# A fused long convolution and Mish MLP on one core: new order of the front, transposing DMAs for ten token tiles, and a column-tiled last hidden chunk

## The chip, the cores and the metric

The kernel runs on one core of one Trainium2 chip. The metric is device time in microseconds (us) of one execution, lower is better. A profiled execution has a span, from its first to its last recorded instruction, and a time of its own, which is a little longer.

## The reference, cut to what matters

S = 2048 tokens, D = 640 channels, F = 1728 hidden units, all bfloat16. Block A is a gated causal long convolution, block B an MLP with the Mish activation, each behind a layer norm and with a residual.

```
k_shift = sum over t<4 of k_pad[:, t:t+S, :] * shift_k[:, 3-t]
kv = k_shift * v
y  = irfft(rfft(pad(kv)) * rfft(pad(ssm_k)))[:S] + kv * ssm_D
h  = q + layernorm(q) * y
h2 = h + mish(layernorm(h) @ w1 + b1) @ w2
```

## The kernel before, in words

**Layout.** Nearly everything lives in one SBUF tile, `arena`, whose regions are byte offsets per partition (`OFF_...`, L108 and on) that are used again by later stages. The framework sets a wait wherever an instruction touches a region that an earlier one, in program order, writes or reads; it looks at the bytes and not at the names.

**Block A, the front.** The convolution is a Fourier transform written as matmuls. The 640 channels are 160 groups of 4 (each two complex pairs), in five chunks `dc` of 128 channels; two wide sets are `KGRP`/`VGRP` = chunks 0, 1, 2 and chunks 3, 4. The filter side: `k1pe`/`k1ev` transpose `ssm_k` into the ring `kk`, `s1kpe` is the first transform stage (L588, L589: two matmuls of 64 output columns, into PSUM partitions 0 to 63 and 64 to 127), `s1kev` its eviction, `s2kpe` the second stage (L616), `kpev` the eviction into the spectrum `KP`. The data side: `kspe` (L667) makes the shifted k of one chunk with 44 matmuls of 64 rows, `kv` (L676, two halves per chunk, DVE) multiplies by v, `s1vpe`/`s1vev` and `s2vpe`/`xev` are the two stages again, and `prod` (L796, DVE) multiplies the data's spectrum into `KP` and into `KPS`. Evictions are L469 on ACT (`copy`) or L471 on DVE.

`KPS` is a copy of `KP` with even and odd partitions exchanged. It is made by 20 DMAs of 256 KB (`d_swap`, L715), twelve for the first set and eight for the second. `KPS` lies over the buffers of the filter and of k (`kn`, `kT`), so a swap waits until the chunks of `kT` under it have been shifted. The inverse is `i1pe` (L807 on `KP`, L808 on `KPS`, eight groups each; set 0 has twelve of them, set 1 eight, `i1pe1_3` reading groups 120 to 127 and `i1pe1_4` groups 128 to 135) with the eviction `i1ev` into `zb`.

**One queue.** All large loads and all swaps are issued by SP in program order: filter chunks, a constant table, v, k (five transposing DMAs, L555), the 20 swaps, the eight loads of q (`d_x`, L740), the table of the last inverse stage (L744), five of w1 (L824), the loads of w2 (L833, and L835 and L836 for its last two chunks, under the one record `d_w2_12`), and at the end 16 output DMAs (L950). An instruction of SP that waits holds up everything behind it.

**Block B, per token tile of 128 tokens (16).** `i2pe` (L859) is the last inverse stage, then `lnx` (L866, ACT), `wb` (L870), `h` (L874), `ln2` (L879) on DVE, the reciprocal root on POOL, and `dr` (L889, DVE) writes the normalized tile into a slot of the ring `hc` (three slots). `trpe` (L896) transposes it with five 128x128 matmuls into PSUM and `trev` evicts it into `lnhT`. Then the MLP runs over units of 128, 128, 256, 512, 512 and 512 tokens. Per unit: 14 hidden chunks `fc`, each with five matmuls over the whole width (`m1pe`, L922) and one Mish on ACT (`hb`, L928); then per token tile 28 matmuls of 320 columns (`m2pe`, L938), the residual on DVE (`res`, L947, ring `ob` of three slots) and the output DMA. Chunk 13 has 64 valid hidden units; its other 64 columns of w1 and rows of w2 are zeros (memsets on POOL). 24 filler matmuls (L907) may be placed ahead of the MLP's start.

**The order.** Every step is a record with an engine, an estimated duration, dependencies and a priority. A list scheduler (`_schedule`, L223) plans them with these costs, taking priorities by name from the dict `PRIO` (L42 to L109); the instructions are emitted in the order of the planned starts, so each engine's queue is fixed by `PRIO`.

PSUM has eight banks: stages of block A take them in four pairs, `i2pe` and `m2pe` share two pairs (0 to 3), and `trpe`, fillers and `m1pe` share the four single banks 4 to 7.

Of the kernel before, what the change touches and what calls it, by code (L numbers as in the profile page):

```python
# [17 lines left out]
D = 640  # L18
FF = 1728
P = 128  # L20
NDC = 5
NDG = 160
NFC = 14
FP = NFC * P
EPS = 1e-5
UNITS = [128, 128, 256, 512, 512, 512]
# [4 lines left out]
def _dgs(groups):  # L31
# [11 lines left out]
    "s1vpe4_1": -1084.07, "s1vev4_1": -895.297, "s1kev0_1": -783.559, "ln1_11": -673.872, "s1kpe0_2": -662.244, "s1vev4_0": -642.027,  # L43
    "d_t2m0": -634.774, "s1vpe4_3": -627.041, "s1vpe4_0": -586.651, "kspe1": -528.715, "trev8": -526.705, "k1ev2_0": -440.311, "dr14": -421.646,
    "prod1_6": -404.891, "d_swap1_1_144": -401.66, "ln2_4": -390.382, "s1v4": -380.868, "s1vev4_2": -378.346, "d_kn2": -376.095, "i2pe1": -364.118,
    "h8": -360.726, "ln2_14": -347.192, "k1ev4_0": -347.08, "d_small": -346.931, "s1vpe0_1": -346.401, "d_t2m3": -343.964, "ln2_12": -343.944,
    "d_x5": -343.772, "lnx3": -337.529, "s2kpe1_5": -334.625, "d_w2_0": -333.608, "d_swap1_1_112": -333.054, "s1vev0_1": -332.909,
    "ln2s_10": -332.519, "i2pe2": -331.875, "k14": -330.872, "i1pe0_11": -325.893, "s1vev0_2": -324.761, "i1ev0_1": -324.375, "s1vpe0_3": -322.854,
    "k13": -321.955, "wb11": -321.583, "s1v0": -321.005, "ln2s_6": -320.994, "k1ev3_1": -318.511, "k1ev3_0": -312.058, "s1vev0_0": -308.301,
    "dadd2": -307.418, "gb0_3": -306.3, "s2vpe1_6": -299.454, "ln1_6": -287.069, "kpev1_7": -281.24, "kpev1_3": -280.517, "gb3_1": -276.187,  # L50
    "ln2s_7": -274.75, "ln2s_15": -271.065, "trpe0": -269.272, "d_w1_3": -269.164, "s2kpe0_0": -269.002, "s2kpe1_7": -268.737, "s2k1": -267.837,
    "s2kpe1_1": -266.674, "kpev1_5": -265.225, "s1kpe0_1": -265.172, "prod0_10": -263.654, "lnx5": -263.473, "kpev0_10": -263.253,
    "kpev0_6": -263.108, "s2kpe1_6": -262.634, "h13": -262.479, "s1k0": -262.447, "d_swap1": -261.002, "s1kpe0_0": -260.487,
    "d_swap1_1_128": -260.376, "d_kn1": -259.944, "s2kpe0_3": -259.426, "kpev1_6": -259.404, "kpev1_0": -258.442, "kpev0_8": -257.822,
    "s2kpe0_1": -256.694, "lnx14": -256.319, "ks1": -256.299, "h5": -256.225, "kpev0_1": -256.172, "k1ev0_1": -255.9, "s2k0": -255.839,
    "xev1_3": -255.756, "s2vpe1_1": -255.473, "lnx6": -255.014, "s2kpe0_5": -254.711, "k10": -254.289, "s2kpe1_4": -254.144, "s2kpe0_2": -254.067,
    "i2pe0": -252.796, "dr13": -252.519, "s2vpe1_7": -252.166, "d_b1": -251.343, "gb3_0": -251.146, "trpe3": -250.749, "s2kpe0_12": -250.46,
    "wb9": -249.953, "s2kpe0_6": -249.105, "ln2s_13": -248.966, "gb3": -248.921, "s2v1": -248.74, "s2vpe1_2": -248.651, "wb1": -247.474,
    "xev1_1": -247.096, "d_x1": -245.444, "kv3_0": -245.276, "xev1_7": -244.982, "prod0_9": -244.689, "s2kpe0_8": -244.221, "ln1f6": -244.145,
    "prod0": -243.097, "xev1_0": -242.979, "ln2_0": -242.897, "prod0_7": -242.718, "kv3": -242.175, "dr9": -242.145, "kv3_1": -239.063,  # L60
    "s2vpe1_5": -238.333, "h10": -237.962, "prod0_3": -237.882, "wb7": -237.561, "ln1_0": -236.799, "wb15": -235.044, "h1": -234.974,
    "ln2s_11": -234.032, "prod0_5": -233.248, "ln1_15": -228.976, "s2kpe0_7": -225.516, "k1pe2": -224.287, "k12": -223.078, "kpev0_9": -222.911,
    "wb8": -210.108, "dadd3": -208, "s1kev0_0": -205.067, "k1pe0": -203.714, "i1pe0_3": -202.801, "s1vev1_2": -190.917, "ln2_5": -174.03,
    "s1kev1_1": -169.397, "ln2s_9": -162.587, "h14": -161.654, "i1pe0_6": -158.89, "s1kpe3_2": -137.753, "kpev1_2": -134.75, "i1ev0_3": -118.959,
    "gb2_3": -113.837, "s2kpe0_9": -101.622, "kpev0_5": -98.7273, "d_swap0_0_48": -97.5315, "h7": -88.2405, "d_kn0": -83.2816, "s1kev0_3": -78.4861,
    "xev0_6": -63.7381, "wb3": -49.867, "d_w2_8": -47.3508, "d_w1_2": -45.5566, "xev0_2": -30.7737, "d_swap1_0_128": -26.7119, "s1kpe4_1": -14.0612,
    "s1kpe1_0": -10.6839, "wb6": -2.5716, "lnx9": -1.3738, "wb0": -0.81, "prod1_4": 2.6876, "prod1_7": 3.4238, "trpe4": 4.7868, "s1vev1_3": 4.8087,
    "lnx11": 5.2768, "prod1": 6.2994, "kv0_1": 7.5174, "wb12": 8.8973, "prod1_5": 9.8603, "kv0": 11.7525, "trev2": 13.2447, "ln1_1": 13.7331,
    "kv2_0": 14.2514, "trev0": 16.0207, "prod1_2": 18.849, "prod0_11": 32.7862, "s1kev2_2": 33.1735, "s1kpe4_3": 36.2703, "s1kev4_0": 37.2914,
    "s2vpe0_3": 41.9142, "h12": 42.0082, "s1k4": 43.0899, "s1kpe4_0": 43.1012, "d_swap1_0_144": 45.428, "ln2_10": 45.7185, "d_R": 48.1646,  # L70
    "h2": 52.836, "ln1_13": 55.0516, "lnx10": 57.3322, "kpev1_1": 58.7842, "d_kn3": 59.2308, "trev1": 59.2408, "d_x4": 62.4421, "k1ev4_1": 62.625,
    "prod0_6": 65.0696, "i1ev0_5": 66.5531, "i1ev0_7": 74.2691, "i2pe7": 76.4684, "s2vpe0_1": 76.9986, "i1pe0_1": 77.7192, "i1pe0_9": 81.1524,
    "i1ev0_8": 81.3582, "i1pe0_10": 81.9868, "i1ev0_10": 82.4371, "i10": 82.5143, "i1ev0_4": 83.02, "trev15": 83.1319, "i1ev0_11": 84.5899,
    "i1pe0_8": 85.8154, "i1ev0_0": 89.9092, "prod0_12": 89.9441, "i1pe0_7": 91.9125, "dadd4": 93.1137, "ln2s_0": 97.9857, "ln2s_4": 101.194,
    "k1ev2_1": 101.992, "i1pe0_5": 109.491, "ln1s0": 115.449, "ln1_2": 116.6, "i2pe3": 117.026, "gb1_1": 117.089, "s1vpe2_3": 119.856,
    "dr15": 119.933, "k1pe3": 120.137, "gb1_0": 123.485, "ln2_15": 123.927, "ks2": 123.947, "s1vpe2_0": 124.485, "s1v2": 124.657, "ln1f8": 125.017,
    "gb1": 125.377, "ln1_10": 125.377, "s1vev2_2": 126.13, "dr11": 128.266, "s1vev2_3": 130.492, "s1k2": 132.203, "trev4": 133.917,
    "s1kpe2_1": 136.795, "ln1f0": 138.935, "dr6": 142.222, "kspe2": 143.3, "kpev0_3": 146.334, "s2kpe0_11": 146.505, "d_t2m1": 147.962,
    "trpe2": 156.415, "ln2_3": 164.617, "s2kpe1_0": 168.186, "kspe3": 177.404, "xev1_5": 177.775, "s2vpe0_9": 178.411, "i2pe4": 188.472,
    "ln2_9": 197.84, "ln2_13": 199.538, "dr0": 205.855, "i2pe5": 207.106, "wb13": 209.871, "trev10": 210.746, "lnx2": 213.249, "trev7": 214.422,  # L80
    "ln2s_8": 214.442, "ln1_12": 215.639, "d_x2": 216.03, "gb1_2": 216.859, "ks3": 217.799, "dr1": 220.849, "prod0_8": 221.875, "d_w2_10": 222.441,
    "h9": 225.267, "s1kev3_1": 227.35, "ln1_5": 229.191, "s2kpe1_3": 237.163, "i1pe1_0": 237.683, "s1kev4_1": 239.657, "i1pe1_4": 241.65,
    "trpe7": 243.277, "d_kn4": 249.69, "d_w2_4": 260.536, "h0": 270.04, "i1ev1_1": 271.196, "wb4": 275.219, "gb3_3": 277.197, "ln2s_5": 278.349,
    "gb2": 279.925, "ln1f2": 281.823, "wb5": 283.209, "prod0_2": 284.452, "i1pe1_6": 287.449, "i1pe0_2": 290.625, "ln1s4": 293.904,
    "s1kpe1_3": 293.926, "d_t2m2": 296.55, "c_diag": 297.586, "h15": 297.926, "trev14": 299.047, "ln1s12": 300.101, "trpe12": 300.344,
    "i2pe6": 300.761, "dr3": 301.674, "d_swap1_0_112": 301.744, "i1ev1_4": 303.196, "d_w2_12": 303.52, "i1pe1_1": 304.622, "ln1f4": 306.066,
    "i1ev1_5": 306.315, "i2pe11": 306.324, "i1ev1_2": 306.74, "ln2s_1": 306.817, "i1pe1_7": 307.432, "d_x0": 307.519, "i11": 307.726, "d_v1": 308.979,
    "ln2_8": 309.852, "gb0_0": 311.166, "i1pe1_5": 312.301, "i1pe1_3": 313.272, "gb2_2": 315.565, "ln1_14": 319.339, "kv1": 319.469, "trpe5": 319.843,
    "gb0": 320.144, "h4": 320.186, "dr5": 320.795, "ln2_2": 320.851, "s1vev3_2": 321.826, "kv1_0": 323.245, "gb0_2": 324.715, "lnx8": 329.755,
    "ln1f12": 330.662, "xev0_10": 330.938, "lnx15": 332.994, "trpe15": 333.927, "wb2": 334.531, "s1kev1_3": 335.515, "d_kT1": 335.56,  # L90
# [34 lines left out]
OFF_W2 = OFF_KPS  # L125
OFF_LNHT = OFF_KP
OFF_UB0 = OFF_KP + 20480
OFF_UB1 = OFF_KPS + 17920
OFF_T2M = OFF_KVB
OFF_LNX = OFF_KVB + 8192  # L130
OFF_HC = OFF_XA
# [872 lines left out]
```

## Time and profile before

| what | value |
|---|---|
| runs | 280.54, 278.85, 279.97 us; median 279.97 |
| profiled execution | its own time 280.54 us, span 278.7 us |
| TensorE clock granted, mean | 0.917 |
| PE busy | 231.0 us, 83% of the span |
| DVE, ACT, POOL busy | 156.1, 138.5, 21.9 us |
| chain that ended last | PE 69%, DMA 8%, ACT 6%, DVE 4%, issue 4% |
| last product of set 0's third chunk to multiply by v (`kv0_1`) ends | 64.7 us |
| first load of q issues | 107.3 us |
| last `i1` eviction ends | 136.5 us |
| first matmul of the MLP | 142.2 us |
| last matmul of the MLP | 274.95 us |

How to read it: times are from the start of the span. A group of instructions is one line of code on one engine, with count, busy time, mean duration of one, and the idle time ahead of them. The chain is followed back from the last instruction, at each step to what released it. SPq is SP's queue, which issues DMAs. A wait line gives the engine's idle time, how often, and the longest.

### The profile page before, as it was taken

How to read it: one execution, taken by the hardware profiler on the slowest of the kernel's cores; microseconds unless marked ns; L12 is line 12 of the kernel's file. 1: busy time of each engine (PE TensorE's matmuls, PEld its weight loads, DVE VectorE, ACT ScalarE, POOL GpSimd, SP SyncE). 2: the span in 40 equal slices, each digit the busy share in tenths (PEclk: the TensorE clock that was granted, in tenths of full speed). 3: DMA queues.
4: the chain of work that ended last, by engine and by line, in shares of the span. 5: the costliest groups of instructions: out<-in, count | busy, mean ns of one | idle time of the engine just before them, and what ended most of it. 6: DMA issues, size and time to landing. Idle time of an engine off the chain costs nothing.

```text
span 278.7 us, 6564 instructions
## 1 busy us (share of the span) xinstructions
PE 231.0 (83%) x2843; PEld 174.2 (63%) x2850; DVE 156.1 (56%) x313; ACT 138.5 (50%) x193; POOL 21.9 (8%) x39
## 2 busy tenths in 40 slices
PE   8890994637912737999999999999999999999994
PEld 4780893526812626899778787645776457744672
DVE  1994485016811658999799898795826711210121
ACT  2691565016901549999769372767403650046200
POOL 2600000000000000002112112012100200000000
PEclk9997799755995668999999999999999999999998
DMA  7999995310032014959500000100011000100011
GB/s 246 416 125 218 168 143 228 151 67 14 4 149 79 14 62 130 303 196 362 184 4 2 24 24 4 47 2 0 24 37 37 2 0 24 49 24 0 2 47 47
DMA packets 20046, 25.48 MB, mean 91 GB/s; under 512 B 11633, under 2 KB 15538, under 8 KB 19634
## 3 DMA queue, kind: packets, MB, share of 16 engines
q1 hardware_dynamic: 19760, 24.88, 31.2%
q8 instruction: 22, 0.36, 0.5%
q10 hardware_dynamic: 146, 0.18, 0.3%
q0 software_dynamic: 112, 0.01, 0.2%
q14 instruction: 6, 0.05, 0.1%
HBM read 14.58 MB, written 2.62 MB: 62 GB/s over the span
## 4 chain that ended last, share of the span: by engine, by line
PE 69%; DMA 8%; ACT 6%; DVE 4%; issue 4%; SPq 2%; ACTq 0%; DVEq 0%
PE banks L938 22%; PE banks L922 22%; DMA arena<-arena 8%; ACT arena L469 6%; PE banks L667 5%; PE banks L616 4%; PE banks L808 3%; PE banks L859 3%; PE banks L807 3%; SPq L715 2%; PE banks L588 2%; PE banks L896 2%; DVE arena L796 1%; DVE arena L676 1%; PE banks L907 1%
## 5 line engine op out<-in xcount | busy, mean ns | idle before, releaser
L469 ACT CAST arena<-banks 128x1024 bf16<-128x1024 f32 (+2 forms) x81 | 74.5, 1021 | 56.7 <-DMA arena<-arena 36.6
L922 PE MATMUL banks<-arena 128*128 128x512 bf16 (+2 forms) x414 | 61.4, 307 | 0.4
L938 PE MATMUL banks<-arena 128*128 128x320 bf16 x448 | 61.7, 299 | 0.0
L928 ACT ACTIVATE arena<-banks,b1s 128x512 bf16<-128x512 f32 (+2 forms) x84 | 43.4, 544 | 35.6 <-PE banks L922 34.4
L938 PEld LDWEIGHTS <-arena 128*128 128x128 bf16 x448 | 43.7, 98 | 16.9
L922 PEld LDWEIGHTS <-arena 128*128 128x128 bf16 x420 | 35.3, 98 | 25.4 <-issue 0.4
L588 PE MATMUL banks<-consts,arena 128*64 128x128 bf16 x320 | 26.1, 240 | 27.6 <-ACT arena L469 14.5
L947 DVE TENSOR_TENSOR arena<-banks,arena 128x640 bf16<-128x640 f32 x16 | 13.2, 823 | 49.4 <-PE banks L938 49.4
L589 PEld LDWEIGHTS <-arena 128*64 128x64 bf16 x320 | 22.0, 124 | 28.7 <-issue 28.6
L616 PE MATMUL banks<-arena 128*128 128x96 bf16 (+1 forms) x512 | 23.4, 206 | 9.7 <-ACT arena L469 9.1
L796 DVE TENSOR_TENSOR arena<-arena 128x960 bf16<-128x960 bf16 (+2 forms) x42 | 25.4, 670 | 10.2 <-DMA arena<-arena 8.2
L676 DVE TENSOR_TENSOR arena<-banks,arena 128x1024 bf16<-128x1024 f32 x10 | 12.0, 1221 | 33.1 <-DMA arena<-arena 24.7
L616 PEld LDWEIGHTS <-arena 128*128 128x128 bf16 x512 | 21.2, 101 | 11.4 <-issue 10.3
L471 DVE CAST arena<-banks 128x1024 bf16<-128x1024 f32 (+3 forms) x23 | 26.0, 1161 | 3.8 <-PE banks L589 1.4
L589 PE MATMUL banks<-consts,arena 128*64 128x128 bf16 x320 | 26.7, 243 | 0.0
L588 PEld LDWEIGHTS <-arena 128*64 128x64 bf16 x320 | 22.7, 123 | 1.5 <-DVE arena L471 0.4
L866 ACT ACTIVATE arena<-arena,nmr_75,r1v 128x640 bf16<-128x640 bf16 x16 | 14.3, 930 | 10.5 <-DVE nmr_75 L761 7.9
L808 PE MATMUL banks<-consts,arena 128*128 128x128 bf16 x160 | 18.7, 219 | 0.8 <-issue 0.4
L807 PE MATMUL banks<-consts,arena 128*128 128x128 bf16 x160 | 18.8, 219 | 0.0
L667 PE MATMUL banks<-diagm,arena 64*128 64x256 bf16 (+3 forms) x220 | 15.2, 311 | 4.0 <-DMA arena<-arena 4.0
L667 PEld LDWEIGHTS <-arena 64*128 64x128 bf16 x220 | 13.2, 155 | 5.9 <-issue 4.4
L807 PEld LDWEIGHTS <-arena 128*128 128x128 bf16 x160 | 15.6, 98 | 0.7 <-issue 0.5
(47 smaller groups left out, 184.8 us busy)
## 6 DMA issues: line engine op xcount, KB each, us to landing
arena<-arena SPq DMA_DIRECT2D x20, 256.0 KB, 2.4
arena<-in_A_ssm_k_dram SPq DMA_DIRECT2D x5, 512.0 KB, 6.4
arena<-in_A_v_dram SPq DMA_DIRECT2D x2, 1280.0 KB, 15.3
arena<-in_A_q_dram SPq DMA_DIRECT2D x8, 320.0 KB, 4.5
out_dram<-arena SPq DMA_DIRECT2D x16, 160.0 KB, 1.8
arena<-in_B_w_dram SPq DMA_DIRECT2D x5, 432.0 KB, 4.3
arena<-in_B_w_dram SPq DMA_DIRECT2D x6, 320.0 KB, 4.8
arena<-tab_R SPq DMA_DIRECT2D x1, 1024.0 KB, 8.3
```

What stands on the lines that cost most here:

```text
L469: clock.append(nc.scalar.copy(o, i))
L471: nc.vector.tensor_copy(o, i)
L588: nc.tensor.matmul(ps1[0:64, gl, :], lhs, fcfs_b[:, 0, :], start=True, stop=True)
L589: nc.tensor.matmul(ps1[64:128, gl, :], lhs, fcfs_b[:, 1, :], start=True, stop=True)
L616: nc.tensor.matmul(ps2[:, c0:c0 + nd], G_t()[:, f0 + fl, :], src[:, f0 + fl, :], start=True, stop=True)
L667: nc.tensor.matmul(outs[h][:, t0:t1, :], lhs, diagm[rows, dc * 4 + t0 - src:dc * 4 + t1 - src, :], start=(src in (-3, 5)), stop=(src in (7 ...
L796: nc.vector.tensor_tensor(kp, x, kp, ALU.mult)
L807: nc.tensor.matmul(pz[:, gl, :], KP_t()[:, dg, :], a12_b[:, 0, :], start=True, stop=False)
L808: nc.tensor.matmul(pz[:, gl, :], KPS_t()[:, dg, :], a12_b[:, 1, :], start=False, stop=True)
L922: nc.tensor.matmul(ph[:, 0:w], w1_t()[:, dc, fc * P:(fc + 1) * P], lnhT_t()[:, dc, c0:c0 + w], start=(dc == 0), stop=(dc == NDC - 1))
L928: nc.scalar.activation(ub_t[u % 2]()[:, fc, 0:w], rt.tile[:, 0:w], ACT.Mish, bias=b1s[:, fc:fc + 1], scale=1.0)
L938: nc.tensor.matmul(po[:, hf2 * 512:hf2 * 512 + 320], hb[:, fc, tl * P:(tl + 1) * P], w2_t()[:, fc, hf2 * 320:(hf2 + 1) * 320], start=(fc = ...
```

## The change

**1. Transposing DMAs.** For token tiles 6 to 15 the five PE transposes and the PSUM eviction are replaced by one transposing DMA on SP from the `hc` slot to `lnhT`. The slot is held until it lands.

**2. Column-tiled last chunk.** In the four units wider than 128 tokens, chunk 13 is computed by ten matmuls of 64 output columns and half the width instead of five of 128 columns and the whole width: the first half of the unit's tokens goes to PSUM partitions 0 to 63, the second to 64 to 127. One Mish of half the width follows. For the second half's tiles `m2pe` takes its last matmul from `w2z`, which has the last 64 rows of w2 in partitions 64 to 127 and zeros in 0 to 63. `w2z` is loaded by one more DMA of SP in the record `d_w2_12` and zeroed by one more memset on POOL; b1's last 64 values are loaded to both halves of the partitions.

`OFF_W2Z` is 73,216. `KPS` starts at 40,960 with 256 bytes per group, so `w2z` (1,280 bytes) lies where `KPS` has groups 126 to 130. In the new program order `d_w2_12` stands behind `i1pe1_6`, `i1pe1_4` and their neighbours and ahead of `i1pe1_3` and `i1pe1_2`, which read groups 120 to 127 and 112 to 119; `i1pe1_3` thus reads groups 126 and 127 after `w2z` was written over them.

**3. Priorities.** The whole dict `PRIO` is new, and so is the order of nearly every step. What moves most:

| place | before | after |
|---|---|---|
| PE, set 0's shifts | `kspe1`, second stage of the filter, `kspe2`, one more of that stage, five of `s1v`, `kspe0` | `kspe1`, second stage of the filter, five of `s1v`, `kspe2`, `kspe0` |
| SP, set 0's swaps: what they wait for | `kv2_1` and a `kpev` (1st), `kspe0` (7th), `kv0_0` (11th) | a `kpev` (1st), `kspe2` (3rd), `kv2_0`, `kspe0` (7th), `kv2_1` (10th), `kv0_0` (12th) |
| SP, set 1's first swap | behind `kspe3`, `prod0_1` and `xev0_9` | behind `kv3_1` and `xev0_10` |
| SP, set 1's other waits | `prod0_9`; `kv3_0`, `xev0_2`; `prod0_6`, `kspe4`, `s1vev3_1`; `prod0_2`, `xev0_12` | `prod0_10`, `kspe4`, `xev0_4`; `xev0_5`; `prod0_4`; `kv4_0`; `xev0_0` |
| SP, first load of q | behind `kv4_1`, `xev0_5` | behind `kv4_1`, `s1vev3_1` |
| SP, last loads of w2 | `d_w2_12` third from the end, then chunks 2 and 6 | `d_w2_12` at the end, behind `i1ev1_6` |
| SP, the end | 16 outputs | outputs and transposes mixed: 0, 1, t7, t6, t8, 2, 3, t10, t9, t13, 4, t14, t12, t15, 5, 6, 7, t11, 12 to 15, 8 to 11 |
| PE, units of the MLP by their tiles | 0; 1; 2, 3; 4 to 7; 8 to 11; 12 to 15 | 0; 1; 2, 3; 4 to 7; 12 to 15; 8 to 11 (its first product between `m2pe14` and `m2pe15`) |

The diff, cut to its core:

```
+XBAR_FROM = 6
+OFF_W2Z = OFF_UB1 + 14336
...
-        nc.gpsimd.dma_start(b1b[0:64, 13:14], B_b1[13 * P:FF].rearrange("(c p) -> p c", c=1))
+        for r in (0, 64):
+            nc.gpsimd.dma_start(b1b[r:r + 64, 13:14], B_b1[13 * P:FF].rearrange("(c p) -> p c", c=1))
...
+    w2z_t = lambda: big("w2z", [P, D], OFF_W2Z)
...
             nc.gpsimd.memset(w2_t()[64:128, 13, :], 0.0)
+            nc.gpsimd.memset(w2z_t()[0:64, :], 0.0)
             nc.sync.dma_start(w2_t()[:, 12, :], B_w2[12 * P:13 * P, :])
-            return nc.sync.dma_start(w2_t()[0:64, 13, :], B_w2[13 * P:FF, :])
+            nc.sync.dma_start(w2_t()[0:64, 13, :], B_w2[13 * P:FF, :])
+            return nc.sync.dma_start(w2z_t()[64:128, :], B_w2[13 * P:FF, :])
...
+        if t2 >= XBAR_FROM:
+            o = DMA(f"d_tr{t2}", 164e3, (lambda e, t2=t2, hc=hc: nc.sync.dma_start_transpose(lnhT_t()[:, :, t2 * P:(t2 + 1) * P], hc.tile)),
+                    w=[("lnhT", t2)], prio=pr, after=[o_dr] + i1_pes, issue=1.3, rate=110e3, xbar=True)
+            hc.users.append(o)
+            continue
...
+            split = fc == NFC - 1 and w > P
+            wp = w // 2 if split else w
...
+                if split:
+                    for dc in range(NDC):
+                        for r in range(2):
+                            nc.tensor.matmul(ph[64 * r:64 * r + 64, 0:wp], w1_t()[:, dc, fc * P:FF],
+                                             lnhT_t()[:, dc, c0 + r * wp:c0 + (r + 1) * wp], start=(dc == 0), stop=(dc == NDC - 1), skip_group_check=True)
+                    return
...
+                half, last = divmod(tl, max(1, nt // 2))
                 for hf2 in range(2):
                     for fc in range(NFC):
-                        nc.tensor.matmul(po[:, hf2 * 512:hf2 * 512 + 320], hb[:, fc, tl * P:(tl + 1) * P],
-                                         w2_t()[:, fc, hf2 * 320:(hf2 + 1) * 320], start=(fc == 0), stop=(fc == NFC - 1))
+                        k = last if fc == NFC - 1 else tl
+                        w2s = w2z_t() if fc == NFC - 1 and half else w2_t()[:, fc, :]
+                        nc.tensor.matmul(po[:, hf2 * 512:hf2 * 512 + 320], hb[:, fc, k * P:(k + 1) * P],
+                                         w2s[:, hf2 * 320:(hf2 + 1) * 320], start=(fc == 0), stop=(fc == NFC - 1))
```

## The prediction

> **What bounds the kernel now.** I read the page's slices first, then the table by stage, then SP's waits and the chain of waits in the front, last the groups by shape and the DMA issues. In the slices (each 7 us) PE is full but for a dip near 21 to 27 us and a long one between 80 and 105 us, and the clock falls there too.
>
> ```profile
> PE   8890994637912737999999999999999999999994
> ...
> PEclk9997799755995668999999999999999999999998
> ```
>
> The table by stage has length, then busy time of PE, PEld, DVE, ACT, POOL, then granted clock, DMA share, GB/s.
>
> ```profile
> 20.92:27.36 6.44, 0.00 (x0) 0.00 (x0) 2.81 (x8) 1.00 (x2) 0.00 (x0) 0.77 1.11 186
> 27.36:31.30 3.94, 3.94 (x49) 3.17 (x48) 0.00 (x0) 1.01 (x1) 0.00 (x0) 0.50 1.22 223
> 64.72:76.98 12.26, 11.79 (x270) 11.05 (x267) 9.57 (x12) 10.06 (x11) 0.00 (x0) 0.83 0.02 3
> 76.98:107.27 30.29, 13.14 (x196) 11.40 (x194) 12.96 (x18) 10.42 (x13) 0.00 (x0) 0.66 0.18 70
> 107.30:136.51 29.21, 26.79 (x528) 25.05 (x529) 26.23 (x48) 28.84 (x32) 2.99 (x8) 1.00 0.84 279
> 122.25:138.50 16.25, 16.20 (x258) 14.69 (x255) 13.39 (x27) 14.39 (x17) 2.44 (x3) 1.00 0.81 275
> 136.51:142.24 5.73, 5.60 (x43) 3.12 (x42) 5.05 (x13) 1.61 (x3) 0.55 (x1) 1.00 0.02 5
> 142.24:274.95 132.71, 132.36 (x1009) 88.30 (x1014) 68.78 (x173) 58.90 (x105) 12.59 (x19) 1.00 0.05 20
> ```
>
> Three regimes follow. From 77 to 107 us nobody is busy: that is the second set's swaps. From 107 to 136.5 us ACT is the bound (28.84 of 29.21 us, 0.913 us per instruction with its gap). From 142.2 us on, PE is, with 0.35 us idle.
>
> ```profile
> SPq L715 <- DVE arena L796: 30.6, 4, 15.2
> ...
> SPq L715 <- DVE arena L676: 10.9, 3, 4.7
> ...
> SPq L715 <- PE banks L667: 5.8, 2, 5.6
> ```
>
> These are waits of SP's queue ahead of a swap. In the chain one sees what a round of such waits is: a swap of 2.37 us lands, an engine that waited for it does its step, and only then the next swap issues.
>
> ```profile
> 76.98 0.47 SPq L715
> ...
> 77.50 2.37 DMA arena<-arena
> ...
> 79.99 1.24 DVE arena L796 x2
> 81.25 0.46 SPq L715
> 81.75 2.36 DMA arena<-arena
> ...
> 86.04 4.28 DMA arena<-arena
> 90.49 0.97 ACT arena L469
> ...
> 92.56 3.62 PE banks L667 x44
> ```
>
> **The change, part by part**
>
> *First set's swaps.* They start some 1.8 us earlier (one shift is no longer ahead of them: 2.12 us in its row at full clock, less a wait). But SP now waits for `kspe2`, `kspe0` with `kv2_0`, `kv2_1`, `kv0_0` and then `kv0_1` ends: five rounds where there were four. A round is 2.37 + 1.24 = 3.6 us, so 64.7 - 1.8 + 3.6 = 66.5; I take 66.2 (bounds: 63.7 if a round is hidden, 68.7 if the shifts of two rounds cost 3.5 us at half clock).
>
> *Until the second set's first swap.* Before, 12.26 us with 11 ACT evictions (1.11 us each). After, the swap stands behind `xev0_10`, and 19 evictions of ACT lie between: 19 x 1.11 = 21.1, so 87.3 us where it was 76.98. More of the work is done by then, so less is left beside the rounds.
>
> *Second set's rounds.* After this swap: second swap's landing 2.9 and `kspe4` 3.0 (2.1 at full clock to 3.6 at half), 5.9; then waits on `xev0_5` 3.4 (2.4 + 0.97), on `prod0_4` 3.6, on `kv4_0` behind two swaps 4.28, on `xev0_0` 3.3, and `kv4_1` 3.6 (2.36 + 1.24): 24.1 us. The first load of q issues at 111.4 us, 4.1 later than before. The swaps between these waits are issued past one another in 0.5 us each and are in the sums.
>
> *ACT's stretch.* `s1vev3_1` ends at about 110.1 (1.3 ahead of the q load, its own swap round being the earlier one). Behind it ACT has 31 instructions: 31 x 0.913 = 28.3, plus 1.7 for `kv4_1` and the first stage behind it (0 to 2.2), so 140.2 without any new wait, 3.7 us later than 136.5.
>
> *The new wait: w2z.* The load of `w2z` lies in groups 126 to 130 of `KPS` and in program order ahead of `i1pe1_3`, which reads 120 to 127. PE must wait until it has landed, with `i1pe1_2`, the fillers, all of `i2pe` and the MLP queued behind it in PE's order. PE would want it at 137.3 (140.2 less two evictions and a matmul step of 1.1). When does it land? Two bounds. By issue: the record's loads wait for `i1ev1_6`, five evictions before the end, at 135.7; it is the third load of the record, at 0.6 us an issue, and the row of 80 KB has 4.7 us to landing: 141.6 to 141.9. By the queue: before, w1 and w2 took 16.25 us from the first w1 load, at 275 GB/s; that load moves to 122.25 + 4.2 = 126.5, and 80 KB more are 0.3: 143.0. The wait is 4.3 to 5.7 us; I take 5.0, so the last `i1` eviction ends at 145.2, 8.7 later than before, all parts up to here together. The cover that the same loads had before (nobody in `i1` read them) is gone.
>
> ```profile
> arena<-in_A_k_dram SPq DMA_TRANSPOSE x5, 6.6
> ...
> arena<-in_B_w_dram SPq DMA_DIRECT2D x1, 80.0 KB, 4.7
> ```
>
> *The clock behind it.* After 6.44 us of idle PE at 21 us the clock fell to 0.50 for 3.94 us. Five idle microseconds near 140 may do the same: two `i1pe` of 16 matmuls and the first `i2pe` at half speed. I take +1.0 (0 to +3, the last if the start of the MLP is slow too). The extra memset of POOL (0.63 us in its row) and the extra load of b1 lie beside work that has long been waiting for SP, at nothing; if POOL were late, it would delay only `w2z`, by 0.6.
>
> *The MLP.* (a) Ten tiles lose five transposes each. In the chain five take 0.28 us (their mean of 219 ns is latency, the pitch is 0.056): 50 x 0.056 = -2.8. One more `i2pe` runs ahead of the MLP: -0.55.
>
> ```profile
> L922 PE MATMUL banks<-arena 128*128 128x512 bf16 x204 | 45.3, 379 | 0.3
> ...
> L896 PE MATMUL banks<-consts,arena 128*128 128x128 bf16 x75 | 5.7, 219 | 0.0
> ```
>
> (b) The last chunk's five matmuls of 512 start every 0.215 us, 5 x 0.215 = 1.08 us. If two matmuls on different column halves run beside each other, as L588 and L589 do (pairs start at 52.07 and 52.08, then 52.13 and 52.13), half of it goes: three units x 0.54 and 0.27 in the 256 one, -1.9. Entering and leaving such a stretch before (L589 to L616 and back) left 0.03 to 0.14 us; eight of those are at most 1.2, but most are the 0.03: -1.6 (bounds 0 to -1.9). (c) New waits of PE: 16 tiles' `i2pe` and `m2pe` share two pairs of banks, and in the new order `i2pe` of later tiles stand between products, so that each waits for a `res` or `wb` (0.82 us) in DVE's queue; the ring `hc` keeps a slot till the DMA lands. 0 to 4.0 us, I take two and a half such waits, +2.0. Sum -2.8 - 0.55 - 1.6 + 2.0 = -3.0 (bounds -5.2 to +0.6).
>
> (d) SP carries ten DMAs more among the outputs. An `out` that waits for its `res` holds up the transposes behind it: t14, t12 and t15 are behind out4. They are needed when `m2pe7` ends, 3 x 3.81 = 11.4 us after `m2pe4`. At 1.8 us (the 160 KB output row) they are there in about 7, at nothing; the dear end is in the rivals. The Trainium skill ("Advanced Engine Details and Errata", X-Bar Transpose) says that on trn2 a transposing DMA is as fast as a regular one; by that nothing is added here, while this trace's transposes from HBM took 6.6 us against 6.4 for plain loads of the same size, with SP held 2.9 us at each. The skill also speaks against (b): "TensorEngine Tiling (Array Packing)", Key Properties, says that a switch of the tiling mode drains the array; if each of eight switches cost a whole pass of 0.22 us by that, 1.8 us would go and the gain with it; the rows above show 0.03 to 0.14.
>
> (e) The tail, residual and last output, stays at 3.75 us.
>
> **Sum.** +8.7 + 1.0 - 3.0 = +6.7: span 278.7 + 6.7 = 285.4, the execution's own time 280.54 + 6.7 = 287.2. The profiled execution was 0.57 above the median of 279.97, so **286.7 us** stands against that median.
>
> **Rivals**
>
> *R1, the other side: the w2z load is there in time.* If SP's loads run earlier or faster than I think, so that it lands by 137.3, PE does not wait and the clock does not fall: 286.7 - 5.0 - 1.0 = 280.7. It decides where the wait is below 2.1 us (280.7 + 2.1 = 282.8, the end of "within 1%"). For it: DMA has idle time before 107 us. Against: the record's own wait on `i1ev1_6` leaves only 1.6 us before PE wants the data, and no load of this size landed in under 4.5 us. 0.09.
>
> *R2, the front's rounds are dearer.* The long dip has a clock of 0.66; if one round more appears, or both shifts and the stages between run at half clock, 3 to 4 us are added: about 290. For it: PE idles longer in each round. 0.12.
>
> *R3, the transposing DMAs are as slow as those of k.* Three issues of 2.0 to 2.9 us (2.4), 5.7 to landing and `res4` 0.8 are 13.7, 2.3 later than the 11.4 that hide them: 289.0, and more if units 4 to 11 wait too. For it: the only transposes in the trace; against: they move 512 KB from HBM, these 160 KB within SBUF. 0.12.
>
> *R4, the column halves do not run beside each other* (the change doesn't do what it says): +1.6, 288.3, inside the forecast's own range. For it: they alternate on one stretch of moving data each; against: the L588 pairs.
>
> **How the numbers follow.** The forecast has 0.62, R4 in it, with its own range 283 to 290. R1 0.09, R2 0.12, R3 0.12; 0.05 is left for a front that loses nothing while the MLP's 5.0 us are all saved, at about 275. A measurement tells 1% (2.8 us) from no change here. Faster: that rest, 0.05. Same: R1, 0.09. Slower: forecast, R2 and R3, 0.86. The range 282.5 to 292 leaves out R1, the rest, and the upper ends of R2 and R3, 0.2 together.
>
> **What would show it.** PE idle ahead of L809/L810 with a DMA from in_B_w_dram as the releaser, 4 to 6 us long, near 138 to 145 us, and a clock below 1 behind it; the second set's first swap near 87 us and the first load of q near 111; fewer than 130 us from the first matmul of the MLP to its last; L897's DMAs with SP held under 1.5 us each. I am wrong if that idle is under 2 us, if the last `i1` eviction ends before 140 us, or if the MLP has gained over 5 us or lost time.

## The result, and the profile after

The changed kernel takes 296.31 us (median of four runs, 294.56 to 297.53) against 279.64 for the kernel before: ratio 1.059, 95% interval 1.0525 to 1.0655, so slower by 5.9%. The prediction was 286.7 us (282.5 to 292): the direction is right, the size less than half. The profiled execution took 297.53 us with a span of 295.6, 16.9 us more than before. Some executions of a kernel take over 1.5% longer than its fastest; the ratios leave these out and the medians in us do not, which matters for experiments 1 and 2, where two of four runs, and the trace of experiment 1, are such.

The page's slices are 7.4 us long now. PE, in tenths of the time busy, has the old dip at 22 to 30 us, the long one in two parts, at 44 to 74 and at 89 to 118, and a new one near 148, where the clock falls too.

```profile
PE   7880973615984412999559999999989999999995
...
PEclk9996697566997555699959999999999999999998
```

The table by stage of the changed kernel, with the columns of the one before (length, busy time of PE, PEld, DVE, ACT, POOL, then granted clock, DMA share, GB/s): set 0's swaps, set 1's swaps up to the first load of q, the wait for `w2z`, the MLP.

```profile
42.35:72.22 29.87, 11.86 (x194) 10.46 (x190) 6.83 (x7) 5.55 (x6) 0.00 (x0) 0.66 0.27 107
...
90.73:117.68 26.95, 8.02 (x108) 7.11 (x110) 4.97 (x7) 4.21 (x5) 0.00 (x0) 0.54 0.20 78
...
145.64:154.44 8.80, 3.01 (x22) 2.53 (x24) 0.00 (x0) 2.02 (x2) 0.00 (x0) 0.61 0.34 103
...
161.28:291.95 130.67, 129.16 (x976) 84.68 (x979) 65.94 (x169) 54.12 (x100) 12.83 (x19) 1.00 0.13 33
```

The first two rows are the finding: 57 us in which no engine is busy for half of the time, with a clock of 0.66 and 0.54. The third is the wait that was predicted. The waits of the steps name the swaps (which are the only DMAs from arena to arena in this stretch), in the kernel before and, longer, in the changed one:

```profile
ACT arena L469 <- DMA arena<-arena: 36.6, 6, 14.4
DVE arena L676 <- DMA arena<-arena: 24.7, 4, 10.7
```

```profile
ACT arena L470 <- DMA arena<-arena: 46.0, 5, 23.3
DVE arena L678 <- DMA arena<-arena: 30.0, 6, 8.0
...
PE banks L669 <- DMA arena<-arena: 11.6, 3, 4.5
DVE arena L798 <- DMA arena<-arena: 11.2, 2, 8.1
```

L470 (before: L469) is an eviction on ACT, L678 (before: L676) the product with v, L669 the shift, L798 the product of spectra. Where the 16.9 us of span are, with what was predicted (ends of steps in us; the last column is how much more of the difference there is than predicted):

| place | before | predicted | after | beyond the prediction |
|---|---|---|---|---|
| set 0: `kv0_1` ends | 64.7 | 66.2 | 72.2 | +6.0 |
| set 1's first swap issues, from there | 12.3 | 21.1 | 18.5 | -2.6 |
| first load of q issues, from there | 30.3 | 24.1 | 26.95 | +2.9 |
| last `i1` eviction ends, from there, without the wait for `w2z` | 29.2 | 28.8 | 29.3 | +0.5 |
| wait for `w2z`, and the clock behind it | 0 | 6.0 | 7.5 | +1.5 |
| first matmul of the MLP, from there | 5.7 | 5.7 | 6.8 | +1.1 |
| last matmul of the MLP, from there | 132.7 | 129.7 | 130.7 | +1.0 |

The wait's 7.5 us is that stage's 8.80 less 1.34, which the same two evictions take in the trace of experiment 1, without it. The remaining front of the changed kernel is 10.4 us longer than before (17.9 less 7.5), where 3.7 was predicted.

### The profile page after: what moved, and what is told of

Its sections match the earlier page's. It is cut to its first block, busy times and chain, and to the rows that moved or that the text cites. A ratio compares the mean times of both kernels' runs of the same rounds, so it can differ in the third digit from the quotient of the medians.

```text
span 295.6 us, 6537 instructions
## 1 busy us (share of the span) xinstructions
PE 231.8 (78%) x2813; PEld 174.2 (59%) x2820; DVE 155.0 (52%) x309; ACT 133.6 (45%) x187; POOL 23.1 (8%) x41
## 2 busy tenths in 40 slices
DMA packets 26879, 27.20 MB, mean 92 GB/s; under 512 B 18402, under 2 KB 22371, under 8 KB 26467
## 4 chain that ended last, share of the span: by engine, by line
PE 52%; DMA 18%; DVE 14%; ACT 8%; issue 5%; SPq 2%; DVEq 0%; ACTq 0%
PE banks L959 21%; PE banks L940 15%; DMA arena<-arena 10%; ACT arena L470 7%; PE banks L669 5%; DMA arena<-in_B_w_dram 4%; DVE arena L472 3%; DMA arena<-tab_R 3%; PE banks L618 2%; DVE arena L798 2%; PE banks L864 2%; PE banks L590 2%; PE banks L809 2%; PE banks L810 2%; SPq L717 1%
## 5 line engine op out<-in xcount | busy, mean ns | idle before, releaser
L470 ACT CAST arena<-banks 128x1024 bf16<-128x1024 f32 (+2 forms) x79 | 73.1, 1020 | 74.7 <-DMA arena<-arena 46.0
L946 ACT ACTIVATE arena<-banks,b1s 128x512 bf16<-128x512 f32 (+2 forms) x84 | 41.7, 539 | 46.1 <-PE banks L940 45.6
L940 PE MATMUL banks<-arena 128*128 128x512 bf16 (+2 forms) x394 | 57.9, 305 | 0.3
L959 PEld LDWEIGHTS <-arena 128*128 128x128 bf16 x448 | 43.7, 98 | 18.1 <-issue 1.4
L590 PE MATMUL banks<-consts,arena 128*64 128x128 bf16 x320 | 27.1, 251 | 27.2 <-DVE arena L678 16.5
L940 PEld LDWEIGHTS <-arena 128*128 128x128 bf16 x400 | 33.3, 98 | 23.4
L591 PEld LDWEIGHTS <-arena 128*64 128x64 bf16 x320 | 23.6, 131 | 24.6 <-issue 24.5
L968 DVE TENSOR_TENSOR arena<-banks,arena 128x640 bf16<-128x640 f32 x16 | 13.2, 824 | 43.4 <-PE banks L959 43.4
L678 DVE TENSOR_TENSOR arena<-banks,arena 128x1024 bf16<-128x1024 f32 x10 | 12.2, 1224 | 39.4 <-DMA arena<-arena 30.0
L798 DVE TENSOR_TENSOR arena<-arena 128x960 bf16<-128x960 bf16 (+2 forms) x42 | 25.2, 665 | 12.0 <-DMA arena<-arena 11.2
L669 PE MATMUL banks<-diagm,arena 64*128 64x256 bf16 (+3 forms) x220 | 15.9, 320 | 19.6 <-DMA arena<-arena 11.6
L472 DVE CAST arena<-banks 128x1024 bf16<-128x1024 f32 (+3 forms) x25 | 28.2, 1159 | 4.9 <-DMA arena<-arena 4.0
L591 PE MATMUL banks<-consts,arena 128*64 128x128 bf16 x320 | 27.6, 253 | 0.0
L590 PEld LDWEIGHTS <-arena 128*64 128x64 bf16 x320 | 24.1, 130 | 5.4 <-DVE arena L678 4.2
L875 DVE TENSOR_TENSOR arena<-banks,arena 128x640 bf16<-128x640 f32 x16 | 13.0, 821 | 26.3 <-PE banks L864 24.4
L669 PEld LDWEIGHTS <-arena 64*128 64x128 bf16 x220 | 14.1, 156 | 21.3 <-issue 12.7
L810 PE MATMUL banks<-consts,arena 128*128 128x128 bf16 x160 | 20.2, 227 | 6.7 <-DMA arena<-in_B_w_dram 6.7
L618 PE MATMUL banks<-arena 128*128 128x64 bf16 (+1 forms) x512 | 23.0, 202 | 2.8 <-ACT arena L470 2.4
L618 PEld LDWEIGHTS <-arena 128*128 128x128 bf16 x512 | 20.5, 100 | 4.8 <-issue 4.0
L810 PEld LDWEIGHTS <-arena 128*128 128x128 bf16 x160 | 16.3, 102 | 7.2 <-issue 7.2
L809 PE MATMUL banks<-consts,arena 128*128 128x128 bf16 x160 | 20.1, 227 | 0.3 <-ACT arena L470 0.3
```

The source lines that it names most:

```text
L470: clock.append(nc.scalar.copy(o, i))
L472: nc.vector.tensor_copy(o, i)
L590: nc.tensor.matmul(ps1[0:64, gl, :], lhs, fcfs_b[:, 0, :], start=True, stop=True)
L591: nc.tensor.matmul(ps1[64:128, gl, :], lhs, fcfs_b[:, 1, :], start=True, stop=True)
L618: nc.tensor.matmul(ps2[:, c0:c0 + nd], G_t()[:, f0 + fl, :], src[:, f0 + fl, :], start=True, stop=True)
L669: nc.tensor.matmul(outs[h][:, t0:t1, :], lhs, diagm[rows, dc * 4 + t0 - src:dc * 4 + t1 - src, :], start=(src in (-3, 5)), stop=(src in (7 ...
```

## Experiments

Every ratio is against the kernel before, on the same chip, with its 95% interval.

### 1. w2z elsewhere

```diff
-OFF_W2Z = OFF_UB1 + 14336
+OFF_W2Z = OFF_KK
```

> The changed kernel with w2z moved to the 8 KB of the ring kk, which nobody uses at that time, so that i1pe1_3 has no load to wait for. Theory (the wait for w2z cost its face, 6.1 us of idle PE and half a microsecond of lower clock): the last i1 eviction ends at 147.7 instead of 154.4 and the time is 289.6 us (288.3 to 291). Rival (the wait lay beside something that is late anyway, such as the loads of w1 and w2 or the first tiles' layer norm): 293 to 296.3. What is left over the kernel before, some 10 us, is then of the front.

Measured: 290.78 us, ratio 1.0329 (1.0188 to 1.047), against 1.059 with the wait; by the ratios 7.3 us less, some 4 us either way. In the traces the last `i1` eviction ends at 148.9 instead of 154.4 (147.7 was expected), though the first load of q was 1.8 us later in this execution, at 119.5. The chain of waits of the changed kernel had this in it:

```profile
145.50 5.58 DMA arena<-in_B_w_dram
...
151.21 0.27 PE banks L810
151.48 0.11 PE banks L809
```

The load issues at 145.50 and lands 5.58 us later, and then the matmuls of the inverse follow each other at 0.11 us, half the pace of 0.055 that the same lines have at full clock. Without the load in the way the last two `i1` evictions follow their neighbours within 1.34 us and the clock stays up. The wait is real and worth about its face; it is not the larger part. That PE waits for the load, and not the load for PE, also says that `i1pe1_3` reads the bytes of `w2z` in place of its groups 126 and 127: the changed kernel leaves out a part of their spectrum, and `w2z` has to be moved for the values as well as for the time.

### 2 and 3. The arena in two tiles, in both kernels

```diff
-    arena = pool.tile([P, OFF_END // 2], BF16, name="arena")
+    arena = pool.tile([P, OFF_G // 2], BF16, name="arena")
+    arena2 = pool.tile([P, (OFF_END - OFF_G) // 2], BF16, name="arena2")
...
-        v = arena[:, off // 2:off // 2 + n]
+        v = arena[:, off // 2:off // 2 + n] if off < OFF_G else arena2[:, (off - OFF_G) // 2:(off - OFF_G) // 2 + n]
```

No step is added, dropped or moved by this in either kernel.

> The changed kernel, same order of all instructions, with the arena cut in two tiles at the byte where the table G begins, so that the swaps' tile holds the spectra, the filter's and k's buffers and nothing of the buffers of kv, of the stages' evictions and of the products' inputs. Theory (in the front, swaps and steps on other bytes wait for each other because the swaps' every-second-partition regions are taken as the whole tile; the new order puts more such steps between swaps): kv0_1 ends 6 to 10 us earlier than 72.2, the first load of q issues at 105 to 109 instead of 117.7, and the time is 286 us (283 to 289). Rival (the front is late because of its order, evictions of ACT ahead of the second set's first swap, not because of these waits): 293 to 296.

> The kernel before with the same cut of the arena and nothing else. Theory (such waits are in the chain of the kernel before too): the second half of the first set's swaps no longer waits for kv0_0 and the evictions, and the second set waits only for products and shifts; kv0_1 ends about 6 us before 64.7, the last i1 eviction 5 to 10 before 136.5, the time is 272 us (269 to 276). Rival (they are hidden beside the true waits, and ACT's stretch sets the end): 278 to 281.

Measured: the changed kernel 274.23 us, ratio 0.9744 (0.9635 to 0.9852), with `kv0_1` at 56.5 and q's first load at 88.3; the kernel before 266.36 us, 0.9508 (0.9401 to 0.9614), with `kv0_1` at 54.6 and the last `i1` eviction at 122.5 instead of 136.5. Both gained more than the theory had said. The waits on swaps that are left, in the changed kernel with two tiles:

```profile
DVE arena L799 <- DMA arena<-arena: 11.9, 3, 5.3
...
PE banks L670 <- DMA arena<-arena: 10.2, 3, 4.5
```

ACT's 46.0 us and the 30.0 of the product with v are gone: these steps touch no byte that a swap touches, and yet they had waited. So the rounds were made in large part of waits between steps that share nothing, and the kernel before had paid about 14 us for them too.

### 4. The other parts under the old priorities

The dict `PRIO` of the kernel before in the changed kernel, and `OFF_W2Z = OFF_KK`.

> The priorities of the kernel before, with the transposing DMAs and the column-tiled chunk of the change, w2z in the bytes of the ring kk; so the front of before and the two other parts. Theory (the parts are worth what was worked out, 50 transposes 2.8 and column halves 1.6, and the front alone made the kernel slower): from the first matmul of the MLP to the last 128.5 us instead of 132.7, the time is 275.6 us (274 to 278). Rival 1 (new waits in the MLP, banks and slots, take the gain back): 279 to 281. Rival 2 (the transposes on SP are late behind outputs): over 281.

Measured: 293.5 us, ratio 1.0547 (1.0446 to 1.0647). Over 281 us, as rival 2 said, but not for its reason. The front is that of the kernel before (last `i1` eviction at 134.2), but the MLP takes 145.6 us, with one wait of 12.5:

```profile
PE banks L941 <- DMA arena<-arena: 12.5, 1, 12.5
```

Its chain of waits shows who is late:

```profile
206.87 0.82 DVE arena L969
...
217.08 2.60 DMA arena<-arena
...
220.24 2.58 DMA arena<-arena
...
222.96 3.15 PE banks L941 x7
```

The inverse's last stage of tiles 8 and on stands behind the second products of tiles 4 to 7 on PE, so the layer norms start only when `res7` frees their banks; 10 us of DVE's work and then two transposing DMAs of 2.6 us, the second behind the first for its slot, have nothing beside them. The two parts don't pay in every order: under the new priorities the MLP takes 130.7 us with them (experiment 5: 130.3), and PE waits for no transposing DMA.

### 5. Both edits in the changed kernel

> The changed kernel with both edits, w2z in the bytes of the ring kk and the arena cut in two tiles. Theory (the two costs are separate, the wait for w2z 6.1 us of span and the swaps' waits 26): the last i1 eviction ends at 122 instead of 128.2, the time is 268 us (266 to 270), and what is left of the change, order, DMAs and column halves together, is level with the kernel before with the same cut, 266.4. Rival (with the front gone the wait for w2z lay beside the loads of w1 and w2, which now bind): 271 to 274.

Measured: 266.38 us, ratio 0.954 (0.9467 to 0.9613), the last `i1` eviction at 123.2. The two costs are separate. With both gone the change is level with the kernel before under the same cut (0.9508).

### 6 and 7. The parts of the MLP

`XBAR_FROM = 16` in the kernel of experiment 5 for the one, `split = False` for the other.

> As e5_w2z_tiles, with the ten later tiles transposed by PE again; the front is the same instruction for instruction. Theory (50 transposes at a pitch of 0.056 us were worth 2.8 us, and PE's new waits gave back about 1): from the MLP's first matmul to its last 2 us more than in e5. Rival 1 (the DMAs' lateness costs what they save): within 0.5 us. Rival 2 (the evictions held PE as well): 4 us or more.

> As e5_w2z_tiles, with the last hidden chunk on 128 columns again and no use of w2z. Theory (column halves run beside each other): from the MLP's first matmul to its last 1.6 us more than in e5 (1.2 to 1.9). Rival (they run one after the other, or each switch drains the array): 0 to 0.4 us more, or less.

Measured: 278.67 us (ratio 0.9968, 0.9923 to 1.0014) and 267.21 us (0.9561, 0.9447 to 0.9676). From first to last matmul of the MLP: 130.3 us in experiment 5, 141.9 without the DMAs, 131.8 without column halves.

The times of experiments 5 and 7 can't be told apart, the traces can. Column halves are worth 1.5 us there, as predicted: 1.0 in the first products themselves, 0.5 in PE's waits at the inverse's last stage, which stands between them. The other run doesn't measure what it was meant to. With ten tiles' PE transposes back, the planner orders the tail anew, and PE waits 6.0 us ahead of transposes for the layer norms of tiles that are late, and more at the inverse's last stage (12.4 us instead of 7.3 from start to start), as in experiment 4. So it shows that the tail's order is worth some 10 us, and not what a transposing DMA saves at equal order. For that there is only a sum. I added the times from the start of one PE matmul to the start of the next, by line, over the whole MLP: transposes take 4.2 us in the kernel before and 2.1 in the changed one, first products 60.6 against 57.5 plus 2.4 for the column halves, the inverse's last stage with its waits 6.7 against 7.7, second products 60.9 against 60.7. The gain is 2.0 us.

### 8. A tile for each set

```diff
-    arena = pool.tile([P, OFF_END // 2], BF16, name="arena")
+    cuts = [0, 24576, OFF_KPS, OFF_KPS + 24608, OFF_G, OFF_END]
+    parts = [pool.tile([P, (b - a) // 2], BF16, name=f"arena{i}") for i, (a, b) in enumerate(zip(cuts, cuts[1:]))]
...
-    KP_t = lambda: big("KP", [P, NDG, P], OFF_KP)
-    KPS_t = lambda: big("KPS", [P, NDG, P], OFF_KPS)
+    KP_t = lambda grp: view([P, VGRP_DG[grp][1] - VGRP_DG[grp][0], P], OFF_KP + 24576 * grp)
+    KPS_t = lambda grp: view([P, VGRP_DG[grp][1] - VGRP_DG[grp][0], P], OFF_KPS + 24608 * grp)
```

> As e5_w2z_tiles, with five tiles in place of two: each set's spectrum and each set's swapped spectrum has its own (set 1 of the swapped one moved by 32 bytes so that k's chunk 0 lies in set 0's tile and the others in set 1's), the MLP's buffers moved inside these tiles. The products of set 0 and the swaps of set 1 then no longer wait for each other. Theory (these waits are what is left of the false ones, 12 us of DVE's and 10 of PE's): the last i1 eviction ends 4 us earlier than in e5, the time is 264 us (261 to 267). Rival (ACT's evictions set the end of the front by now): less than 1.5 us earlier.

Measured: 254.07 us, ratio 0.9096 (0.9015 to 0.9176); the last `i1` eviction at 111.7, 11.4 us earlier than in experiment 5, where 4 was expected. DVE's waits on swaps are all gone; of PE's, before two shifts, 6.5 us are left.

### 9 and 10. The same waits, undone by order alone

One arena again, and `w2z` in free bytes. The swaps are moved in the program order (9: those of set 0 alone, those ahead of `kv2_1` put just behind it; 10: both sets, behind `kv0_1` and `kv4_1`). The edit of experiment 10:

```diff
+    for pre, last in [('d_swap0', 'kv0_1'), ('d_swap1', 'kv4_1')]:
+        cut = 1 + [o.name for o in order].index(last)
+        moved = [o for o in order[:cut] if o.name.startswith(pre)]
+        order = [o for o in order[:cut] if not o.name.startswith(pre)] + moved + order[cut:]
```

> The kernel of e1 (the change, w2z in free bytes, one arena), with one move in the program order: the ten swaps of set 0 that stood ahead of kv2_1 are put just behind it, so that kspe2, kspe0 and kv2 have no swap ahead of them. Theory (in set 0 each step that stands between swaps costs a round of swap, wait, step; the three rounds of kspe2, kspe0 with kv2_0, and kv2_1 go): kv0_1 ends at 62 to 65 instead of 72.9, the time is 282 us (279 to 285). Rival (the swaps merely start later and the set's end stays): 288 to 291.

> As e9, with all twelve swaps of set 0 behind kv0_1 and all eight of set 1 behind kv4_1, two blocks with nothing between, on one arena. Theory (the swaps act as barriers only by what stands between them): no round is left in set 1 either, the first load of q issues at 98 to 103 instead of 119, and the time is 271 us (267 to 275), without any cut of the arena. Rival (all that stands behind a block waits for its last swap, and this costs what the rounds did): 279 to 283, as e9.

Measured: 281.45 us, ratio 1.0025 (0.9984 to 1.0065), with `kv0_1` at 63.2; and 263.92 us, 0.9383 (0.9307 to 0.946), with the first load of q at 93.0. The chain of experiment 9 has ten swaps issued one behind the other, 0.6 us apart but for one pair at 1.1 (the last of them is the first line here), and after them only the two rounds that still have a step between:

```profile
53.93 0.59 SPq L717
...
54.62 3.50 DMA arena<-arena
...
58.40 1.24 DVE arena L678
...
59.69 2.23 DMA arena<-arena
```

Compare the rounds of the changed kernel, in its chain of waits:

```profile
42.62 4.26 DMA arena<-arena
...
46.92 2.75 PE banks L669 x39
...
51.48 2.37 DMA arena<-arena
...
54.10 3.66 PE banks L669 x44
...
63.27 3.99 DMA arena<-arena
...
67.39 1.24 DVE arena L678
```

Landing and step by turns; with the two rounds left out here (before `kv2_1` and `kv0_1`) there are five. A swap costs as a barrier by what stands between it and the next one. With `w2z` out of the way, moving ten swaps by a few places takes the changed kernel back to the time of the kernel before; moving all twenty, which gave more than was expected, beats both with the same arena.

### 11 and 12. Five tiles with blocks, and five tiles in the kernel before

The loop of experiment 10 with `kspe0` and `kspe4`, on the kernel of experiment 8; and the edit of experiment 8 alone on the kernel before.

> As e8_set_tiles, with the swaps of set 0 that stood ahead of kspe0 put behind it and those of set 1 that stood ahead of kspe4 behind that. Theory (the two shifts are the last steps that wait for swaps of other bytes, 9 us of PE): the last i1 eviction 3 to 4 us earlier, 251 us (248 to 253). Rival (the swaps' later start takes it back): 253 to 256.

> The kernel before with the five tiles of e8 and nothing else. Theory (with true waits alone the two orders are level in the front, and the change has 2.3 us in the MLP less 1.7 ahead of it): 255 us (252 to 259). Rival 1 (the new order is better where it is not held up): over 259. Rival 2 (the old one is): under 252.

Measured: 252.69 us, ratio 0.8973 (0.8904 to 0.9042), and 255.6 us, 0.907 (0.9002 to 0.9139). PE waits for no swap any more in 11, but at the last `i1` eviction (111.3) this gave 0.4 us where 3 to 4 were expected, and 11 isn't told from 8. DVE now waits 4.7 us for the first load of q (2.3 in experiment 8), which SP issues behind the last swap, at 82.2, and ACT stands idle for 5.0 us behind that: the wait has moved. The kernel before with the tiles is level with the changed one with the tiles.

### 13 and 14. Which partitions a swap touches

Real parts in partitions 0 to 63, imaginary ones in 64 to 127; R's table and the rows of the inverse's constants permuted alike. One arena, every swap where it was.

```diff
-                    ENG_Q[Q_SWAP].dma_start(KPS_t()[half::2, g0:g0 + 16, :].rearrange("p g f -> p (g f)"),
-                                            KP_t()[1 - half::2, g0:g0 + 16, :].rearrange("p g f -> p (g f)"))
+                    ENG_Q[Q_SWAP].dma_start(KPS_t()[64 * half:64 * half + 64, g0:g0 + 16, :].rearrange("p g f -> p (g f)"),
+                                            KP_t()[64 - 64 * half:128 - 64 * half, g0:g0 + 16, :].rearrange("p g f -> p (g f)"))
```

> The kernel of e1 (the change's order, w2z in free bytes, one arena, swaps where the change has them), with the rows of the spectrum put in another order: all real parts in partitions 0 to 63, all imaginary ones in 64 to 127 (the columns of G and the rows of the inverse's constants permuted alike), so that each swap copies 64 neighbouring partitions and not every second one. Theory (a region of every second partition is taken to reach over more than its bytes, and that alone makes the waits): the swaps wait for shifts and spectra only, as in e8 or better, and the time is 254 us (250 to 258). Rival 1 (the waits come from the size of the swaps or the sharing of one arena): 286 to 291 as in e1. Rival 2 (the waits go, but a copy between the two halves of the partitions is slower than the 2.4 us of one over all, or G is slower to build): 259 to 270.

> The kernel before with the same other order of rows and nothing else. Theory: with true waits alone the old order is level with the new one, as in e12 against e8: 255 us (251 to 259). Rival 1 (without tiles the old order is the better one): under 250. Rival 2 (the swaps get slower): 260 to 271.

Measured: the changed kernel (with `w2z` in free bytes) 250.97 us, ratio 0.898 (0.8925 to 0.9036); the kernel before 245.95 us, 0.879 (0.8766 to 0.8814), the fastest version here. In neither does any step between 30 and 115 us wait for a swap. This settles the cause: same arena, same order, same sizes, and the waits are gone when a swap's region is 64 neighbouring partitions. So what was said ahead of the prediction, that the framework looks at the bytes, did not hold for regions of every second partition: with them it also set waits between steps with no byte in common. Both sets' swaps in the fastest version, and ACT's stretch:

```profile
41.00:73.80 32.80, 27.71 (x692) 25.36 (x692) 28.65 (x36) 27.81 (x32) 0.00 (x0) 1.00 0.71 163
73.80:101.80 28.00, 26.04 (x518) 24.60 (x519) 26.05 (x48) 27.98 (x31) 2.99 (x8) 1.00 0.86 291
```

From the first swap's issue to the first load of q it takes 31.7 us (42.2 to 73.9), where the kernel before took 65.1 (42.1 to 107.3), and the clock is full. The expectation for 14 was missed on the good side (rival 1): without the waits the old order reaches the last `i1` eviction at 101.8, 9.0 us ahead of the new one (110.8), and its MLP is 2.4 us longer.

## Why the prediction was right in direction and wrong in size

**First set's swaps: the step that failed.** "five rounds where there were four. A round is 2.37 + 1.24 = 3.6 us, so 64.7 - 1.8 + 3.6 = 66.5; I take 66.2". There were five rounds, but `kv0_1` ended at 72.2, outside the bounds of 63.7 to 68.7; this is 6.0 of the 10.2 us by which the span missed. The rounds didn't start 1.8 us earlier: the first swap issues at 42.00 against 42.13, for the eviction that it waits for is as late as before. And from there to the end of `kv0_1` it took 30.2 us against 22.6, so the added round cost 7.6 us and not 3.6. The rounds of the kernel before:

```profile
45.85 2.38 DMA arena<-arena
...
48.58 3.52 PE banks L667 x44
...
53.90 2.39 DMA arena<-arena
...
56.37 1.24 DVE arena L676
57.66 2.25 DMA arena<-arena
60.13 1.02 ACT arena L469
61.17 2.21 DMA arena<-arena
```

One of these four has a shift in it; of the five after, two have (2.75 and 3.66 us, where a `kv` takes 1.24). And two landings after took 4.26 and 3.99 us, not 2.37. I had priced one added round by the cheapest kind of round and left the other four at what they were.

The long landings are not the price of two swaps behind one wait, as the prediction had read its 4.28: in the changed kernel the pairs issued at 90.73 and 91.25 and at 104.27 and 104.78 had landed 2.35 us after their second issue. The traces show another thing beside them. In the two kernels every swap that took over 2.5 us to land (2.88 to 4.36) has a 16 KB transfer of the queue "q8 instruction" under way beside it, and no swap that landed within 2.41 us has one. The changed kernel has such transfers at 43.1, 63.9 and 109.7 us, beside its landings of 4.26, 3.99 and 4.36. That they are the cause was not tried.

**Until set 1's first swap.** 21.1 us was too much, 18.5 it was: ACT's instructions took 0.93 us each with their gaps (20 in 18.51), as in the stretch where ACT is the bound, and not the 1.11 of the stretch that I had taken.

**Second set's rounds.** 26.95 us instead of 24.1. The one before `xev0_0` took 5.6, where I had written 3.3: its one swap is the third of the long landings. The others were within 0.8, that of `kv4_0` (4.19 against 4.28) by luck: it was a landing of 2.34 and a step of 1.24, and the 4.28 was a long landing without its step.

**ACT's stretch.** 29.3 us against 28.8: right.

**w2z.** The wait and the clock behind it were 7.5 us against 6.0; the mechanism and the place were as foretold, the landing (5.58 us after its issue, where the row had 4.7) was later, and experiment 1 took the wait away.

**The MLP.** -2.0 us against -3.0. By the sums above the transposes gave 2.1 (2.8 foretold), the first products with their column halves 0.7 (1.6 foretold, 1.5 in experiment 7), and the inverse's last stage with PE's waits took 1.0. Not foretold is that the start ahead of the MLP grew by 1.1 us. Some 0.6 of it is there in every run of the new order without the wait (6.35 against 5.73): it is about the one `i2pe` that the prediction took off the MLP (-0.55) and should have put on here, for it was moved and not saved.

**The rivals.** R2, dearer rounds, comes nearest to what happened, with no round more than forecast, at 6.7 us instead of its 3 to 4 and with the 0.12 that I gave it. R1 fell: PE waited 6.7 us for the load. R3 did not occur in the changed kernel: the DMAs held SP for 1.2 us each and PE waited for none of them. R4 fell by experiment 7.

**What was not asked.** Both profiles list evictions on ACT and products with v that wait for a swap. The prediction counted these waits and never asked which byte they were about; no byte was. The count of rounds would have been the same, but the question would have shown that the order alone sets their number, and that every step put between two swaps is dear.

The Trainium skill, "Advanced Engine Details and Errata", X-Bar Transpose, has transposing DMAs as fast as regular ones on trn2. Here one of 160 KB within SBUF landed after 2.6 us, where a plain copy of 256 KB within SBUF lands after 2.4 and an output of 160 KB, which leaves SBUF, after 1.8, so by the measurement it is slower; in the changed kernel PE waited for none of them. The skill's "TensorEngine Tiling (Array Packing)", Key Properties, has a switch of the tiling mode drain the array. Forty matmuls on column halves took 2.4 us. The twenty whole ones in their place would be 15 x 0.215 + 5 x 0.109 = 3.8, an estimate from the rows' pitch, and what went from the first products is 3.1 (60.6 less 57.5), which leaves 0.7 us for eight switches, under 0.1 each: if there is a drain, it is nearer to the rows before (0.03 to 0.14) than to a pass.

**What stays open.** What a transposing DMA saves at the same order of everything else was not isolated. Whether the framework takes every region with a step between partitions for its whole tile, or only some, was not tried; shown is that the waits go with the step. What makes some landings long was not tried either.

## What to carry to other kernels

When a profile shows an engine waiting for a DMA, ask which byte the two share; if none, the wait may come from how the region is described (here a step of two between partitions), and describing it otherwise, cutting the tile, or moving such DMAs together may take it away; here this was worth 12% and 5 to 9% in the kernel before, and the moving brought the changed kernel to 6% under it. A chain of "transfer, wait, step" is priced by each of its rounds and not by the cheapest, with the clock that went with its idleness here (0.54 to 0.66 where PE was busy for 30 to 40% of the time, 1.00 in experiment 14 where it was for over 80%), and one more step between two transfers is one more round. A buffer put into bytes that someone has still to read puts its whole transfer into the path (here 80 KB cost 7.5 us) and overwrites what is to be read.

## What the runs showed of the hardware that was not expected

A swap between the two halves of the partitions took longer to land than one between odd and even ones, 4.9 and 5.5 us in the median of experiments 13 and 14 against 2.4, though there the swaps also follow each other closely, so the cause is open; no step waits for it. The transposing DMAs within SBUF:

```profile
L897 SPq DMA_TRANSPOSE arena<-arena x10: 1199/1206/1932, 188.5 to 250.6; - x10
...
DMA to landing us min/median/max: 2.6/2.6/4.1
```

SP is held for 1.2 us at each, against 2.9 in the median for k's from HBM in the kernel before, and the packets under 512 bytes rose from 11,633 to 18,402 in all, some 680 for each.
